# Loads of a second expert group moved ahead of a w2 load, and copies reordered in the first attention head

## The chip, the cores and the metric

One NeuronCore of a Trainium2 chip runs the whole program. The metric is the device time of one execution in microseconds (us); lower is better. The kernel before took 422.44 us (median of 3 runs, 422.02 to 424.92). The execution whose profile is read below took 423.74 us, and the span from its first to its last instruction is 421.9 us.

## The reference

Three layers are computed in a row, all in float32:

```
attention (2 x 8 heads, 768 steps, head size 64):
    state = gamma_h * state + outer(k_t, v_t);   y_t = (q_t . state) / 8
dense layer on x = y, [2, 768, 512]:
    h = relu(x @ w_in)                           # 512 -> 1024
    c = 3-tap convolution of h along the sequence, per channel
    x = (h * sigmoid(c)) @ w_out                 # 1024 -> 512
experts (8): logits = x @ w_gate, a sigmoid gate decides whether a token
    takes its own best expert or its predecessor's;
    out = p[e] * (relu(x @ w1[e]) @ w2[e])       # 512 -> 1024 -> 512
```

## The kernel before

**Attention.** Two heads share the 128 partitions, so there are 8 pairs ("heads" in the code), each cut into 6 slices of 128 steps. For each slice TensorE computes scores `s_ps` (line 284), VectorE multiplies them by a decay table into `at` (286), and two slices later TensorE adds the state (`inc`, 292) and computes the output `y` from `at` and the values `vz` (304) and from q and the state (306). Before this, `prepare` (line 244) makes operands of each head: q copied into a zero-padded tile `qz` (253 on VectorE, 255 on ScalarE), q times its decay on GpSimd (258), k times its decay (263 on VectorE for the first head's second half, 265 on ScalarE), and the values copied into the zero-padded `vz` (`values`, 279, ScalarE). Only the first head comes in two parts, slices 0 and 1 and slices 2 to 5, so that it can start before all of it is loaded. `prepare` is a generator; the main loop over slices (line 444) calls `advance`, which takes one step of each running generator when its counter comes to zero. What the loop writes first stands first in each engine's queue; the engines take their queues strictly in this order.

**Dense layer.** Its matmuls (lines 134 to 136, three passes on split high and low words) start inside the attention loop and then run on their own until 235 us.

**Experts.** Tokens are sorted by expert into tiles of 128 rows; 11 tiles are always run (`experts`, line 968). What is left over from the experts goes in groups of four quarters of 32 rows (`group`, 902), of which two are always run. For tile j, `fetch(j, 0)` loads w1 (2 MB in 4 loads of 512 KB, line 715), `fetch(j, 1)` loads w2; `cut` (732) splits the words on ScalarE (738) and VectorE (739), `g1` and `g2` multiply. For j > 1 a load carries a condition read on the chip: where the tile two before used the same expert, it moves nothing. A group needs 8 pieces of weights of 2 MB each (4 of w1, 4 of w2, each piece 4 loads, line 729), which go alternately into two slots, `qc` and `qs1l`; a piece can be loaded only when TensorE has used up what stood in its slot. `hook` (line 960) is called four times a tile, and at the numbers in `QT` it takes one step of the group; group 1 has its steps at hooks 21, 26, 30, 30, 31, 35 and 40. Hook 26 comes at the end of tile 5, hook 30 at the end of tile 6; each multiplies two pieces (924) and then asks for the next two. All weight loads are issued by the SP queue, in the order in which the loop writes them, and every load there waits until the load eight places before it has landed (eight semaphores are used in turn).

Of the kernel before, what the change touches and what calls it, by code (L numbers as in the profile page):

```python
# [92 lines left out]
def tile_kernel(ctx, tc, cat, cst, qT, kT, kN, vN, w_in, conv_w, w_out, wg, w1, w2, out):  # L93
# [116 lines left out]
    def keep_busy(n):  # L210

        for _ in range(n):
            te.matmul(idle[:, 0:P], zst[0], zst[0], start=True, stop=True)
# [9 lines left out]
    class Head:  # L223
# [21 lines left out]
        def prepare(self):  # L245
            hp = self.hp
            qd = ca[:, hp, C_QD:C_QD + CH]
            for c in self.parts:
                t = slice(c.start * CH, c.stop * CH)
                for j in range(2):  # L250
                    pj = slice(64 * j, 64 * j + 64)
                    if len(self.parts) > 1 and j:
                        ve.tensor_copy(out=self.qz[pj, j, t], in_=self.kq[pj, 1, t])  # L253
                    else:
                        se.activation(out=self.qz[pj, j, t], in_=self.kq[pj, 1, t], func=AF.Copy)
                    yield 1
                q1 = self.q1[:, c.start:c.stop]
                po.tensor_tensor(out=q1, in0=q1, in1=qd.unsqueeze(1).to_broadcast([P, len(c), CH]), op=ALU.mult)
                for j in range(2):
                    k1 = self.kv[:, 0, c.start:c.stop, 64 * j:64 * j + 64]  # L260
                    kd = ca[:, hp, C_KD + j:C_KD + j + 1]
                    if len(self.parts) > 1 and j:
                        ve.tensor_scalar(out=k1, in0=k1, scalar1=kd, scalar2=None, op0=ALU.mult)
                    else:
                        se.activation(out=k1, in_=k1, func=AF.Copy, scale=kd)
                    if len(self.parts) > 1:
                        self.values(c, j)
                    yield 1

            if len(self.parts) == 1:  # L270
                yield 1
                for c in (range(3), range(3, 6)):
                    for j in range(2):
                        self.values(c, j)
                    yield 3
# [40 lines left out]
    def load(p):  # L316
        heads[p] = Head(p // 4, p % 4, p % 2)

    def small():
        w = yield from narrow(cw_words, 24)  # L320
        se.activation(out=cw.rearrange("p m t -> p (m t)"), in_=w, func=AF.Copy)
        ve.tensor_copy(out=identr, in_=ident)
        ve.tensor_copy(out=sel, in_=cs[0:RK + E, R_SEL:R_SEL + 10])
# [95 lines left out]
    running, done = [], []  # L419

    def advance():
        for r in list(running):
            r[1] -= 1
            if r[1] <= 0:
                r[1] = next(r[0], 0)
                if not r[1]:
                    running.remove(r)
# [6 lines left out]
    start = heads[0].prepare()  # L434
    for _ in range(4):
        next(start)
    running.append([start, 1])
    rest = None
    LOOK = 2
    LOADS = {1: 2, 11: 3, 15: 4, 20: 5, 28: 6, 32: 7}  # L440
# [3 lines left out]
    for i in range(len(seq) + LOOK):  # L444
        if i < len(seq):
            p, c = seq[i]
            heads[p].scores(c)
            if i == 0:
                keep_busy(8)
            if c == 0 and p + 1 < 8:  # L450
                running.append([heads[p + 1].prepare(), 2])
            if i in STARTS:
                running.append([convert(*parts.pop(0)), 1])
            if i in LOADS:
                load(LOADS[i])
            if i == 14:
                running.append([small(), 1])
        todo = rest
        if i >= LOOK:
            p, c = seq[i - LOOK]  # L460
            rest = heads[p].output(c)
        if todo:
            todo()
        advance()
        while i >= FIRST and slices[0] < (i - FIRST + 1) * RATE:
            next(first)
            slices[0] += 1
# [227 lines left out]
    def expert_at(n):  # L695
        return sy.value_load(ei[0:1, 0, n:n + 1], min_val=0, max_val=E - 1)

    def raw(lane, which):
        if (lane, which) not in RAW:
            RAW[lane, which] = (wx if lane and which else ws).tile([P, 4, 1024], F32, name=f"r{lane}{which}")  # L700
        return RAW[lane, which]

    def fetch(j, which, parts=range(4)):

        src = (w1, w2)[which].rearrange("e p a n -> e p (a n)")
        kw = {}
        if j == 0:
            src = src[0]
        else:
            src = src[bass.ds(expert_at(j), 1)].rearrange("o p n -> (o p) n")  # L710
            if j > 1:
                kw = dict(cond=sy.value_load(ei[0:1, 1, j:j + 1], min_val=0, max_val=1), cond_hint=True)
        dst = raw(j % 2, which)
        for i in parts:
            sy.dma_start(out=dst[:, i, :], in_=src[:, i * 1024:(i + 1) * 1024], **kw)
# [120 lines left out]
    def begin_x(j):  # L836

        x, X[j] = X[j], psb.tile([P, 4, P], F32, tag="b", name="tp")
        for k in range(4):
            te.matmul(X[j][:, k, :], x[:, k * P:(k + 1) * P], ident, start=(k == 0), stop=False, skip_group_check=True)  # L840
        late_x(j, 0)
# [45 lines left out]
    def finish(j, last=False):  # L887
        if last:
            yo = wk.tile([P, F], F32, tag="hr", name="yo")[:, 0:DM]
        elif j >= NTILE:  # L890
            yo = wk.tile([P, F], F32, tag="hq", name="yo", bufs=1)[:, 0:DM]
        else:
            yo = wk.tile([P, DM], F32, name="yo", bufs=1)
        se.activation(out=yo, in_=Y.pop(j), func=AF.Copy, scale=pr[:, j:j + 1])  # L894
        po.indirect_dma_start(out=rows_of[j], out_offset=bass.IndirectOffsetOnAxis(ap=it[:, j:j + 1], axis=0),  # L895
                              in_=yo, in_offset=None, bounds_check=NT - 1, oob_is_err=False)

    def tile_g1():
        return [psa.tile([P, 512], F32, tag=f"a{n}", name="g1") for n in range(2)]
# [55 lines left out]
    QT = [3, 5, 10, 10, 11, 15, 20] + [21, 26, 30, 30, 31, 35, 40]  # L955
    groups = []
    hooks = [0]

    def hook():
        hooks[0] += 1  # L960
        while QT and QT[0] <= hooks[0]:
            QT.pop(0)
            while groups and next(groups[0], done) is done:
                groups.pop(0)

    def experts(n):

        fetch_q(0, 0, 1)
        fetch(1, 1)
        for j in range(2):  # L970
            begin_x(j)
        for j in range(2):
            turn_x(j)
        gather(NTILE)
        gather(2)
        groups.extend(group(g, g + 1 < QSTAT) for g in range(QSTAT))
        h = tile_g1()
        for i in range(2):
            g1(0, i, h)
            cut(1, 0, i)  # L980
            if i:
                relu(0, h)
            hook()
        cut(0, 1, 0)
        fetch(2, 0)
        T = {}
        for j in range(n):
            last, ahead = j + 1 == n, j + 2 < n
            behind = j + 3 < n and j > 0 and hooks[0] + 1 in QT
            if j + 3 < n and not behind:  # L990
                fetch(j + 3, 0)
            if j > 0:
                finish(j - 1)
            if j + 3 < n:
                gather(j + 3)
            if j == 2:
                gather(NTILE + 1)
            if j not in T and j > 0:
                T[j] = turn_h(j)
            if not last:  # L1000
                h = tile_g1()
                g1(j + 1, 0, h)
                if j == 0:
                    T[j] = turn_h(j)
                    cut(0, 1, 1)
                if ahead:
                    cut(j + 2, 0, 0)
                hook()
                if behind:
                    fetch(j + 3, 0)  # L1010
                g1(j + 1, 1, h)
                if ahead:
                    cut(j + 2, 0, 1)
                relu(j + 1, h)
                hook()
            if ahead:
                turn_x(j + 2)
                fetch(j + 2, 1)
            Y[j] = y = psb.tile([P, 512], F32, tag="b", name="y")
            for i in range(2):  # L1020
                g2(j, i, T[j], y)
                if not last:
                    cut(j + 1, 1, i)
                    if not ahead and i == 0:
                        T[j + 1] = turn_h(j + 1)
                    hook()
        finish(n - 1, True)
        assert not QT

# [68 lines left out]
```

## Time and profile before

| what | value |
|---|---|
| time, median of 3 runs | 422.44 us |
| time of the profiled execution | 423.74 us |
| its span | 421.9 us |
| TensorE matmul busy | 406.2 us (96%) |
| VectorE, ScalarE, GpSimd busy | 290.3, 256.1, 92.7 us |
| bytes moved by DMA | 86.57 MB |
| granted TensorE clock, mean | 0.996 |

The busy time of TensorE is modelled from the starts of its matmuls, so a matmul that waits for part of its data may still count as busy. That is why the rows below show single stretches in order of time: from one row's start to the next one's start is what the step took.

### The profile page before, as it was taken

The page shows a single profiled execution, that of the slowest core. Times are in us where ns is not written, and L with a number is a line of the kernel's source. Part 1 is how long each engine was busy: PE and PEld are TensorE (multiplying, and loading weights), DVE is VectorE, ACT ScalarE, POOL GpSimd, SP SyncE. Part 2 cuts the span into 40 slices and gives each one's busy share as a digit, 9 for nine tenths or more (in the row PEclk, how much of TensorE's full clock was granted, in tenths as well). Part 3 has the DMA queues.
Part 4 walks back from the last instruction along what each step waited for, and adds up shares of the span by engine and source line. Part 5 has one row for each costly group of instructions (what it writes and reads, how often), then busy time and mean ns, then how long its engine had stood idle before and what let it go on. Part 6 is the DMA issues. An engine that isn't in the chain of part 4 may idle for free.

```text
span 421.9 us, 7069 instructions
## 1 busy us (share of the span) xinstructions
PE 406.2 (96%) x2412; PEld 329.5 (78%) x2412; DVE 290.3 (69%) x494; ACT 256.1 (61%) x405; POOL 92.7 (22%) x92
## 2 busy tenths in 40 slices
PE   8999999999999999999999999999999998999992
PEld 7898999999987889988778886767667764676671
DVE  3789989798973621678995387968595957285550
ACT  2787778578663333667313487869586846485550
POOL 5356756230100000000004130341131320200110
PEclk9999999999999999999999999999999999999998
DMA  7989871320000101000486999999978969658301
GB/s 238 389 295 405 276 246 54 106 89 6 2 2 0 75 27 50 2 0 2 174 294 198 372 406 331 381 412 401 403 285 302 361 244 402 237 218 299 151 31 42
DMA packets 27322, 86.57 MB, mean 205 GB/s; under 512 B 3598, under 2 KB 4622, under 8 KB 27280
## 3 DMA queue, kind: packets, MB, share of 16 engines
q1 hardware_dynamic: 25200, 79.76, 51.1%
q0 software_dynamic: 2080, 6.29, 4.1%
q8 instruction: 21, 0.34, 0.3%
q14 instruction: 21, 0.17, 0.1%
HBM read 105.18 MB, written 6.55 MB: 265 GB/s over the span
## 4 chain that ended last, share of the span: by engine, by line
PE 38%; issue 34%; POOL 10%; DVE 8%; ACT 4%; DMA 3%; SPq 1%; POOLq 0%
PE x_ps L134 6%; PE x_ps L135 5%; PE x_ps L136 5%; POOL out_dram L895 4%; POOL xg L748 4%; PE h_ps L134 3%; PE y L304 3%; PE h_ps L135 3%; PE s_ps L284 3%; PE h_ps L136 3%; DVE cc L367 3%; DMA xs<-xl 2%; PE y L306 2%; DMA kq<-in_qT_dram 1%; ACT cc L364 1%
## 5 line engine op out<-in xcount | busy, mean ns | idle before, releaser
L134 PE MATMUL h_ps<-xT,wih 128*128 128x384 f32 x128 | 46.1, 360 | 0.1
L895 POOL DMA_INDIRECT out_dram<-yo,it x13 | 16.4, 1262 | 134.8 <-ACT yo L894 134.8
L367 DVE SCALAR_TENSOR_TENSOR cc<-h,cw,cc 128x768 f32<-128x768 f32 x32 | 34.9, 1091 | 15.2 <-ACT cc L364 15.1
L748 POOL DMA_INDIRECT xg<-xs,it x13 | 18.4, 1418 | 121.8 <-DVE ei L683 107.9
L135 PE MATMUL h_ps<-xT,wih 128*128 128x384 f32 x128 | 43.1, 337 | 0.0
L136 PE MATMUL h_ps<-xT,wil 128*128 128x384 f32 x128 | 43.1, 336 | 0.0
L134 PE MATMUL x_ps<-woh,hg 128*128 128x512 f32 x96 | 38.6, 402 | 0.0
L135 PE MATMUL x_ps<-wol,hg 128*128 128x512 f32 x96 | 37.5, 391 | 0.0
L136 PE MATMUL x_ps<-woh,hg 128*128 128x512 f32 x96 | 37.5, 391 | 0.0
L739 DVE TENSOR_TENSOR ws1h<-r,ws1h 128x1024 fp32r<-128x1024 f32 x22 | 26.0, 1222 | 12.8 <-ACT ws1h L738 9.3
L155 POOL TENSOR_TENSOR na<-na,raw 128x512 int32<-128x512 int32 (+1 forms) x17 | 23.0, 1354 | 50.8 <-DVE na L153 25.7
L739 DVE TENSOR_TENSOR wc<-r,wc 128x1024 fp32r<-128x1024 f32 x22 | 26.0, 1221 | 11.7 <-ACT wc L738 11.6
L738 ACT ACTIVATE wc<-r 128x1024 fp32r<-128x1024 f32 x22 | 22.1, 1055 | 14.6 <-PE g L136 14.6
L304 PE MATMUL y<-at,vz 128*128 128x128 f32 x192 | 29.5, 275 | 0.9 <-ACT vz L279 0.9
L284 PE MATMUL s_ps<-qz,kq 128*128 128x256 f32 x96 | 29.0, 385 | 1.0 <-DVE qz L253 1.0
L739 DVE TENSOR_TENSOR ws0h<-r,ws0h 128x1024 fp32r<-128x1024 f32 x22 | 26.0, 1222 | 5.6 <-ACT ws0h L738 5.5
L739 DVE TENSOR_TENSOR ws0l<-r,ws0l 128x1024 fp32r<-128x1024 f32 x22 | 26.0, 1222 | 5.1 <-ACT ws0l L738 5.0
L304 PEld LDWEIGHTS y<-at,vz 128*128 128x128 f32 x192 | 25.9, 192 | 1.5 <-ACT vz L279 1.1
L738 ACT ACTIVATE ws0l<-r 128x1024 fp32r<-128x1024 f32 x22 | 22.1, 1053 | 7.7 <-PE y L136 7.7
L286 DVE TENSOR_TENSOR at<-s_ps,ca 128x256 f32<-128x256 f32 x48 | 20.2, 421 | 8.4 <-PE s_ps L284 7.7
L134 PEld LDWEIGHTS h_ps<-xT,wih 128*128 128x128 f32 x128 | 24.1, 189 | 1.9 <-issue 1.2
L506 ACT ACTIVATE xn<-x_ps 128x512 f32<-128x512 f32 x10 | 6.0, 598 | 32.0 <-PE x_ps L136 13.8
(234 smaller groups left out, 1042.4 us busy)
## 6 DMA issues: line engine op xcount, KB each, us to landing
r<-in_w_dram SPq DMA_DIRECT2D x88, 512.0 KB
qc<-in_w_dram SPq DMA_DIRECT2D x32, 512.0 KB
qs1l<-in_w_dram SPq DMA_DIRECT2D x32, 512.0 KB
raw<-in_w_in_dram SPq DMA_DIRECT2D x8, 512.0 KB
raw<-in_w_out_dram SPq DMA_DIRECT2D x8, 512.0 KB
kq<-in_qT_dram SPq DMA_DIRECT2D x7, 384.0 KB
kq<-in_kT_dram SPq DMA_DIRECT2D x7, 384.0 KB
kv<-in_vN_dram SPq DMA_DIRECT2D x7, 384.0 KB
```

Of the source, the lines that this page charges most:

```text
L134: te.matmul(ps, lhi, rhi, start=first, stop=False)
L135: te.matmul(ps, lhi, rlo, start=False, stop=False)
L136: te.matmul(ps, llo, rhi, start=False, stop=last)
L155: po.tensor_tensor(out=a, in0=a, in1=lo, op=ALU.add)
L284: te.matmul(ps, self.kq[:, 0, tok], self.qz[:, :, tok], start=True, stop=True)
L286: ve.tensor_tensor(out=self.at[c], in0=ps, in1=self.dm, op=ALU.mult)
L304: te.matmul(y, vz[:, c, j, :], at[:, j, :], start=(j == 0), stop=(c == 0 and j == 1))
L367: ve.scalar_tensor_tensor(out=cc, in0=h[:, i:i + S], scalar=cw[:, m, i:i + 1], in1=cc, op0=ALU.mult, op1=ALU.add)
L738: se.activation(out=w[:, 0, h, :], in_=r, func=AF.Copy)
L739: ve.tensor_tensor(out=w[:, 1, h, :], in0=r, in1=w[:, 0, h, :].bitcast(F32), op=ALU.subtract)
L748: return po.indirect_dma_start(out=xg, out_offset=None, in_=xs[0:n], in_offset=bass.IndirectOffsetOnAxis(ap=it[:, j:j + 1], axis=0), bound ...
L895: po.indirect_dma_start(out=rows_of[j], out_offset=bass.IndirectOffsetOnAxis(ap=it[:, j:j + 1], axis=0), in_=yo, in_offset=None, bounds_ch ...
```

## The change

Three edits. In `experts`, the w2 load of tile j + 2 is put behind the second multiplication of tile j where only the second group is left and its next step falls on the hook after the next one. That is so for tiles 5 and 6 (hooks 26 and 30), so `fetch(7, 1)` and `fetch(8, 1)` move. In `prepare`, the two copies of values of the first head stand ahead of its k times decay. In the main loop, the two copies of q of the first head's second part are taken right after the first scores instead of after the first and the second slice; the counter 3 keeps the later steps where they were.

```
-    running.append([start, 1])
+    running.append([start, 3])
...
             if i == 0:
                 keep_busy(8)
+                for _ in range(2):
+                    next(start)
...
                 po.tensor_tensor(out=q1, in0=q1, in1=qd.unsqueeze(1).to_broadcast([P, len(c), CH]), op=ALU.mult)
+                for j in range(2 if len(self.parts) > 1 else 0):
+                    self.values(c, j)
                 for j in range(2):
...
-                    if len(self.parts) > 1:
-                        self.values(c, j)
                     yield 1
...
             if ahead:
                 turn_x(j + 2)
-                fetch(j + 2, 1)
+                after = len(groups) == 1 and hooks[0] + 1 not in QT and hooks[0] + 2 in QT
+                if not after:
+                    fetch(j + 2, 1)
...
                     hook()
+            if ahead and after:
+                fetch(j + 2, 1)
```

The SP queue at tile 5, before: `r00` is w1 of tile 8, `r11` is w2 of tile 7, `qc4` and `qs1l` are the third and fourth w1 piece of group 1, `r10` is w1 of tile 9. The TENSOR_LOADs read the expert and the condition.

```order
L715 DMA r00_2027<-in_w1_dram 128x1024
L696 TENSOR_LOAD ei_1427
L696 ISA x2
L712 TENSOR_LOAD ei_1427
L712 ISA x2
L715 ISA
L715 DMA r11_2465<-in_w2_dram 128x1024
...
L729 DMA qc4_3689<-in_w1_dram 128x1024
...
L729 DMA qs1l_3702<-in_w1_dram 128x1024
...
L715 DMA r10_2037<-in_w1_dram 128x1024
```

The same place with the change:

```order
L717 DMA r00_2027<-in_w1_dram 128x1024
L731 ISA
L731 DMA qc4_3667<-in_w1_dram 128x1024
...
L731 DMA qs1l_3680<-in_w1_dram 128x1024
...
L698 TENSOR_LOAD ei_1427
L698 ISA x2
L714 TENSOR_LOAD ei_1427
L714 ISA x2
L717 ISA
L717 DMA r11_2465<-in_w2_dram 128x1024
...
L717 DMA r10_2037<-in_w1_dram 128x1024
```

The four loads of `r11` moved behind the eight loads of the two pieces. At tile 6 the four loads of `r01` (w2 of tile 8) move likewise.

ScalarE in the first head, before (`qz_104` and `qz_105` belong to the first and the second head; 2x64 and 4x64 are the first and the second part):

```order
L255 ACTIVATE qz_104<-kq 64x512
L255 ACTIVATE qz_105<-kq 64x768
L265 ACTIVATE kv<-kv,ca 128x4x64
L279 ACTIVATE vz<-kv 128x4x64
L255 ACTIVATE qz_105<-kq 64x768
L311 ACTIVATE xT<-y 128x256
L279 ACTIVATE vz<-kv 128x4x64
```

With the change:

```order
L255 ACTIVATE qz_104<-kq 64x512
L255 ACTIVATE qz_105<-kq 64x768
L279 ACTIVATE vz<-kv 128x4x64 x2
L267 ACTIVATE kv<-kv,ca 128x4x64
L255 ACTIVATE qz_105<-kq 64x768
L311 ACTIVATE xT<-y 128x256
```

Both copies of values now stand ahead of k times decay; before, the second one stood behind another head's copy and an output.

VectorE in the first head, before:

```order
L263 TENSOR_SCALAR kv<-kv,ca 128x2x64
L286 TENSOR_TENSOR at<-s_ps,ca 128x256 x2
L253 COPY qz_104<-kq 64x512
L286 TENSOR_TENSOR at<-s_ps,ca 128x256
L297 COPY st_108<-inc 64x64 x2
```

With the change:

```order
L265 TENSOR_SCALAR kv<-kv,ca 128x2x64
L286 TENSOR_TENSOR at<-s_ps,ca 128x256
L253 COPY qz_104<-kq 64x512
L286 TENSOR_TENSOR at<-s_ps,ca 128x256 x2
L297 COPY st_108<-inc 64x64 x2
```

The copy of q's second part now stands ahead of the second slice's scores times decay.

## Rows read from the trace of the kernel before

**Rows 1.** Windows: stretch, its length, busy us (count) by engine, clock, DMA share, GB/s
```profile
15.00:45.00 30.00, 28.90 (x208) 26.84 (x207) 27.11 (x80) 22.35 (x51) 16.84 (x13) 1.00 0.92 335
340.00:363.00 23.00, 21.54 (x100) 12.22 (x99) 11.42 (x11) 10.97 (x15) 1.99 (x3) 1.00 0.81 305
```

**Rows 2.** Timeline of PE, hooks 30 and 35: start, us, what [idle before]
```profile
352.84 1.83 PE L924 MATMUL hq_ps<-qc,xq 128*32 128x512 f32 x6
354.89 1.48 PE L924 MATMUL hq_ps<-qc,xq 128*32 128x512 f32 x9 [0.22 <-DMA qc<-in_w_dram]
...
358.20 2.15 PE L924 MATMUL hq_ps<-qs1l,xq 128*32 128x512 f32 x4 [0.98 <-DMA qs1l<-in_w_dram]
360.55 1.90 PE L924 MATMUL hq_ps<-qs1l,xq 128*32 128x512 f32 x10 [0.20 <-DMA qs1l<-in_w_dram]
362.38 1.09 PE L826 MATMUL tp<-cs,hr 128*128 128x128 f32 x8
...
366.07 1.03 PE L826 MATMUL tp<-cs,hq 128*128 128x128 f32 x8
...
379.32 1.92 PE L946 MATMUL yq_ps<-qc,tq 128*32 128x512 f32 x16
...
382.89 0.50 PE L134 MATMUL g<-wc,xh 128*128 128x512 f32 x1
```

**Rows 3.** Waits of PEld, whole run: total us, times, longest
```profile
PEld hq_ps L924 <- DMA qs1l<-in_w_dram: 5.0, 5, 1.9
```

**Rows 4.** Timeline of SP's issues, tiles 4 to 6
```profile
327.79 15.01 SPq L715 DMA_DIRECT2D r<-in_w_dram  x12
343.09 2.44 SPq L729 DMA_DIRECT2D qc<-in_w_dram  x4
345.79 4.29 SPq L729 DMA_DIRECT2D qs1l<-in_w_dram  x4
```

**Rows 5.** Tile r on SP, windows 327:339.5 and 340:343: ns min/median/max, first and last start
```profile
L715 SPq DMA_DIRECT2D r<-in_w_dram x8: 73/73/84, 327.8 to 338.7; - x8
...
L715 SPq DMA_DIRECT2D r<-in_w_dram x4: 311/341/387, 340.4 to 342.5; - x4
```

**Rows 6.** Timeline of ACT around hook 30
```profile
352.94 2.00 ACT L738 ACTIVATE ws0l<-r 128x1024 fp32r<-128x1024 f32 x2 [0.55 <-PE y L136]
362.49 1.09 ACT L930 ACTIVATE hq<-hq_ps 128x512 f32<-128x512 f32 x2 [7.54 <-PE hq_ps L924]
363.46 0.69 ACT L894 ACTIVATE yo<-y,pr 128x512 f32<-128x512 f32 x1
```

**Rows 7.** The page's GB/s in 40 slices of 10.55 us
```profile
GB/s 238 389 295 405 276 246 54 106 89 6 2 2 0 75 27 50 2 0 2 174 294 198 372 406 331 381 412 401 403 285 302 361 244 402 237 218 299 151 31 42
```

**Rows 8.** Timeline of PE, first head
```profile
9.27 0.67 PE L284 MATMUL s_ps<-qz,kq 128*128 128x256 f32 x2 [1.02 <-DVE qz L253]
...
12.48 0.46 PE L292 MATMUL inc<-kv 128*128 128x128 f32 x2
...
14.10 0.49 PE L304 MATMUL y<-at,vz 128*128 128x128 f32 x2 [0.94 <-ACT vz L279]
...
14.65 0.60 PE L284 MATMUL s_ps<-qz,kq 128*128 128x256 f32 x2
```

**Rows 9.** Timeline of DVE, first head
```profile
8.74 0.42 DVE L253 COPY qz<-kq 64x512 f32<-64x512 f32 x1
```

**Rows 10.** Timeline of ACT, first head
```profile
7.82 0.63 ACT L255 ACTIVATE qz<-kq 64x512 f32<-64x512 f32 x1 [1.06 <-DMA kq<-in_qT_dram]
10.78 0.84 ACT L255 ACTIVATE qz<-kq 64x768 f32<-64x768 f32 x1 [2.34 <-DMA kq<-in_qT_dram]
11.54 0.49 ACT L265 ACTIVATE kv<-kv,ca 128x256 f32<-128x256 f32 x1
11.93 0.40 ACT L279 ACTIVATE vz<-kv 128x256 f32<-128x256 f32 x1
```

**Rows 11.** Timeline of SP, the load that waits for k's second part
```profile
8.49 0.33 SPq L431 DMA_DIRECT2D cs<-in_cst_dram  x1
```

## The prediction

> **What bounds the kernel now.** I read the windows first. TensorE is busy 28.90 of 30 us between 15 and 45 us [rows 1], and the same holds, with the clock at 1.00, up to 340 us: TensorE is the bound, and the others keep up. What delays TensorE at one place therefore delays the end by the same, unless a later wait takes it back. So I then looked for places where TensorE waits. The waits of TensorE and of its weight loads name a DMA into `qs1l` as the largest, 5.0 us in 5 waits [rows 3]; the window from 340 to 363 holds most of it (21.54 busy of 23, and weight loads at 12.22) [rows 1]. The timeline shows it plainly. At hook 30 the two pieces are multiplied from 352.84 to 362.38, which is 9.54 us. At hook 35 the same number of matmuls of the same shape takes 382.89 - 379.32 = 3.57 us [rows 2]. So **5.97 us are lost at hook 30**, and the idle gaps beside these rows (0.22, 0.98, 0.20) hide most of it, because a matmul that has started counts as busy. The rows also tell what it waits for: the last load of `qc` lets it go on at 354.89, loads of `qs1l` at 358.20 and 360.55.
>
> Why are these pieces late? The SP queue issues them at 343.09 and 345.79 [rows 4]. Ahead of them stand twelve tile loads. Eight take 73 to 84 ns to issue and the last four 311 to 387 ns [rows 5]; the eight move nothing (their expert is the one already there), and the four, from 340.4, are w2 of tile 7. So from 340.4 on twelve loads of 512 KB are under way, 6.3 MB; w2 goes first, and the pieces land behind it.
>
> In the first head TensorE waits twice: 1.02 us before the third scores, for VectorE's copy of q, and 0.94 us (from 13.16 to 14.10) for ScalarE's copy of values [rows 8].
>
> **The change, part by part.** *The w2 load of tile 7.* Without it in front, SP reaches the first piece right after the last of the eight empty loads, 338.7 [rows 5], plus 0.4 for one issue: 339.1. Its slot is free then, because hook 26 has used `qc` up by 338; `qs1l` is free at 340.4, before its turn. Now the landings, by count, from the twelve loads of the trace: the 8th (last of `qc`) is seen at 354.89, 14.5 us after the first issue at 340.4; the 10th at 358.20, 17.8 us; the 12th at 360.55, 20.15 us [rows 2, 5]. With the change the eight piece loads come first, so the last lands at 339.1 + 14.5 = 353.6. The matmuls of the second piece begin at 352.84 + 1.8 (half of 3.57) = 354.6. So both pieces are there, with 1 us to spare, and the step takes 3.57 us: it ends at 356.4 instead of 362.38. **Gain 5.97.**
>
> What is late next is w2 itself. Its last load lands at 339.1 + 20.15 = 359.25. It is needed for a multiplication only some 8 us after hook 30, but its `cut` stands in ScalarE's queue ahead of the group's `hq`, of tile 6's output `yo` and of all the rest. Before, that cut ran at 352.94 [rows 6]. Now its second half starts at 359.25 and takes 1.0; then `hq` 1.09 and `yo` 0.69 [rows 6]: 362.0. TensorE meanwhile does transposes and the first half of tile 8, 3.69 us (362.38 to 366.07 [rows 2]), to 360.1, and wants to transpose `hq`. The second four transposes, 0.4 later, need the PSUM bank that `yo` empties (four banks go round). So TensorE waits from 360.5 to 362.0: **loss 1.5**. Bounds for this loss: 0 if w2 lands by 357.8, since 1.5 less is wanted; 3 if it lands as much later than reckoned. I take 1.5, which the count of landings gives. VectorE's half of the cut ends by 361.6 and stays hidden, as do the extra transposes of tile 7's h.
>
> The Trainium skill (DMA: Bandwidth & Descriptors, Anatomy of one DMA) fits a DMA as about 2.0 us plus its bytes over 436 GB/s. For these 6.3 MB that is an estimate of 16.4 us where the rows have 20.15; by it w2 would land at 355.5, the loss would vanish, and the sum below would be 6.7. The rows decide; the page is for a queue other than SP's.
>
> *The w2 load of tile 8* (moved at hook 30) has the same condition as the empty loads: the issues of tiles 6 and 8 moved nothing [rows 5]. Nothing is transferred, so it costs and brings nothing, and the pieces for hook 35 are issued some 6 us earlier.
>
> *q's copies.* VectorE's copy now runs when q's second part has landed, 7.82 (there ScalarE starts its own [rows 10]), and takes 0.42 [rows 9], to 8.24; ScalarE's ends at 8.45; k's second part has landed by 8.49, since SP's load there waits for it [rows 11]. So the third scores start at 8.55 instead of 9.27: 0.7 sooner. GpSimd's multiply follows by as much. Scores of the second slice times decay come at 8.29 as before, behind the copy.
>
> *Copies of values.* ScalarE's order is now two copies, then k times decay, all behind the second head's q copy that ends at 11.6 [rows 10]. At about 0.4 and 0.4, then 0.49, k's product ends at 12.85, so `inc`, at 12.48 before [rows 8], comes at 12.9. The second copy of values is then long there, and the wait to 14.10 goes. From `inc` to the second pair of `y` it takes 0.5 to 0.7, and from there to the next scores 14.65 - 14.10 = 0.55. These scores start between 13.9 and 14.15 instead of 14.65: a gain of 0.5 to 0.8 in all, not the sum of both waits, because a new wait of about 1.4 us on k's product takes the place of the second. I take **0.7**. It is kept, for up to 340 us everything is started by TensorE's progress; VectorE at 27.11 of 30 us [rows 1] may cost some of it.
>
> **Sum.** 5.97 - 1.5 + 0.7 = 5.2 us. From the profiled execution's 423.74 that is 418.5; that run lies 1.3 above the median of 422.44, so against the median **417.2 us**.
>
> **Rivals.**
> 1. *The order of issue does not matter*, since 16 engines share all loads that are under way; the pieces then land as late as before, and only the first head gains: 422.44 - 0.7 = 421.7. Against it: the landings in the trace follow the order of issue, 354.89, 358.20, 360.55. The Trainium skill (same page, Queues, rings and completion order) says that a ring's descriptors are consumed in order but that completion is not first in, first out; the first half is what the rows show. 6%.
> 2. *The new wait on w2 is larger*, by 1.2 to 3.5 us, as ScalarE stands still in order and every us of w2's delay after 357.8 is a us of TensorE's: 418.4 to 420.7, say 419.5. For it: SP has only eight loads under way, and w2's wait for landings of pieces. 14%.
> 3. *Slower than before.* The same stop of ScalarE, from the point where w2's last load lands after 364.4 (5.2 us later than reckoned). It would if the loads ran at the 244 GB/s of the slice from 337.5 to 348 [rows 7]: 6.3 MB take 25.8 us, with 2 for the rest 27.8, so 366.9 and a loss of 7.65 more: 424.9. Against it: that slice holds idle stretches; from 340 to 363 the mean is 305 GB/s [rows 1], which gives 20.6 us, as counted. 3%.
> 4. *More than forecast*: w2 lands early enough, nothing is lost, and the first head gains 0.8 to 1.5: 414.8 to 415.5. 7%.
>
> **How the numbers follow.** The forecast, 415.6 to 418.4, has 70%; what remains is in the rivals. The likeliest case gives 417.2. The range from 415.3 to 419.4 holds the forecast, about half of rival 2 and some of rival 4, some 80%. A measurement of this kernel tells about 1% from no change, so faster means below 418.2 and slower above 426.7: faster 0.75 (forecast nearly whole, rival 4), within 1% 0.23, slower 0.02.
>
> **What would show it.** In the profile after: hook 30's pair of pieces in about 3.6 us with no DMA wait, SP issuing `qc` at about 339 and w2 of tile 7 after both pieces; ScalarE's second cut of w2 at about 358 to 360 ended by a DMA; a TensorE wait of about 1.5 us before the second transposes of `hq`, released by `yo`; the third scores at 8.5 and `inc` at 12.9 released by ScalarE's k product (all late times earlier by the head's gain). Hook 30 still at 9 us would make rival 1 right. A wait for w2 by the multiplication itself, or pieces late at hook 35, would show steps that I left out.

## The result: about 1% faster, with 4.4 us gained in the profiled execution where 5.2 were forecast

The changed kernel took **418.88 us** (median of 8 runs, 417.41 to 421.46) beside 422.69 us for the kernel before (8 runs, 422.02 to 424.92). The ratio on record is 0.9893, with a 95% interval of 0.9868 to 0.9918; the quotient of the two medians is 0.9910, which is 3.8 us. The forecast was 417.2 us, in a range from 415.3 to 419.4: the median lies in the range, 1.7 us above the forecast. The profiled execution took 419.32 us, its span is 417.5 us, and the mean granted clock is 0.993. Against the profiled execution of before (423.74 us, span 421.9) that is 4.4 us less, where 5.2 were forecast.

### The profile page after: what moved, and what is told of

The parts are those of the page before. It is cut to its first block, busy times and chain, and to the rows that moved or that the text cites. A ratio compares the mean times of both kernels' runs of the same rounds, so it can differ in the third digit from the quotient of the medians.

```text
span 417.5 us, 7069 instructions
## 1 busy us (share of the span) xinstructions
PE 401.6 (96%) x2412; PEld 328.9 (79%) x2412; DVE 290.2 (69%) x494; ACT 256.4 (61%) x405; POOL 93.8 (22%) x92
## 4 chain that ended last, share of the span: by engine, by line
PE 39%; issue 33%; POOL 10%; DVE 8%; ACT 4%; DMA 3%; SPq 1%; POOLq 0%
PE x_ps L134 6%; PE x_ps L136 5%; PE x_ps L135 5%; POOL xg L750 4%; POOL out_dram L897 4%; PE h_ps L134 3%; PE y L304 3%; PE h_ps L135 3%; PE s_ps L284 3%; PE h_ps L136 3%; DVE cc L367 3%; PE y L306 2%; DMA xs<-xl 2%; DMA kq<-in_qT_dram 2%; ACT cc L364 1%
## 5 line engine op out<-in xcount | busy, mean ns | idle before, releaser
L750 POOL DMA_INDIRECT xg<-xs,it x13 | 19.6, 1509 | 121.2 <-DVE ei L685 107.6
L134 PE MATMUL h_ps<-xT,wih 128*128 128x384 f32 x128 | 46.1, 360 | 0.1
L897 POOL DMA_INDIRECT out_dram<-yo,it x13 | 16.4, 1263 | 130.1 <-ACT yo L896 130.1
L740 ACT ACTIVATE ws0h<-r 128x1024 fp32r<-128x1024 f32 x22 | 22.3, 1064 | 7.7 <-DMA r<-in_w_dram 5.4
```

The lines of the kernel that those rows point to most:

```text
L134: te.matmul(ps, lhi, rhi, start=first, stop=False)
L740: se.activation(out=w[:, 0, h, :], in_=r, func=AF.Copy)
L750: return po.indirect_dma_start(out=xg, out_offset=None, in_=xs[0:n], in_offset=bass.IndirectOffsetOnAxis(ap=it[:, j:j + 1], axis=0), bound ...
```

## The profile after

First the windows that answer to [rows 1]. The columns are the same; the last row is a stretch that the prediction passed over.

```profile
15.00:45.00 30.00, 28.89 (x207) 26.86 (x207) 27.39 (x81) 23.41 (x53) 17.56 (x14) 1.00 0.91 336
...
340.00:363.00 23.00, 21.59 (x124) 15.39 (x124) 12.03 (x12) 13.38 (x19) 2.42 (x4) 1.00 1.00 383
...
230.00:300.00 70.00, 68.89 (x399) 50.89 (x398) 48.71 (x48) 48.27 (x63) 17.17 (x16) 1.00 0.99 378
```

From 340 to 363 us TensorE runs 124 matmuls instead of 100 in the same 23 us, and weight loads are busy for 15.39 us instead of 12.22. TensorE's busy time (21.59 and 21.54) says nothing about it, because a matmul that waits half-way counts as busy: **count the matmuls, not the busy share**. The DMA engines are now full in that stretch (1.00 and 383 GB/s, before 0.81 and 305).

The timeline of TensorE around hook 30 answers to [rows 2]:

```profile
352.54 1.92 PE L926 MATMUL hq_ps<-qc,xq 128*32 128x512 f32 x16
354.28 1.90 PE L926 MATMUL hq_ps<-qs1l,xq 128*32 128x512 f32 x16
356.11 1.09 PE L828 MATMUL tp<-cs,hr 128*128 128x128 f32 x8
...
360.96 0.66 PE L828 MATMUL tp<-cs,hq 128*128 128x128 f32 x4 [1.00 <-ACT hq L932]
362.03 0.66 PE L828 MATMUL tp<-cs,hq 128*128 128x128 f32 x4 [0.41 <-ACT yo L896]
362.44 0.48 PE L134 MATMUL g<-wc,xh 128*128 128x512 f32 x1
```

The pair of pieces is multiplied in 356.11 - 352.54 = 3.57 us without a wait, where it took 9.54. The new wait stands behind it, where the prediction put it: the eight transposes of `hq` came in one piece before, and now come in two halves, the first released by ScalarE's `hq`, the second by `yo`.

What ScalarE did meanwhile, answering to [rows 6]:

```profile
355.61 2.26 ACT L740 ACTIVATE ws0h<-r 128x1024 fp32r<-128x1024 f32 x2 [5.40 <-DMA r<-in_w_dram]
358.19 2.24 ACT L740 ACTIVATE ws0l<-r 128x1024 fp32r<-128x1024 f32 x2 [0.32 <-DMA r<-in_w_dram]
360.33 1.07 ACT L932 ACTIVATE hq<-hq_ps 128x512 f32<-128x512 f32 x2
361.29 0.69 ACT L896 ACTIVATE yo<-y,pr 128x512 f32<-128x512 f32 x1
```

The wait before each half of w2's cut is now ended by a DMA. ScalarE stood idle for 5.40 us for the first half. `hq_ps` was there from about 356 on, but `hq` was copied only at 360.33, behind both halves. The cut's last instruction ran from about 359.4 (the row's end less one instruction of 1.06), `hq` and `yo` behind it.

The issues of SP, answering to [rows 4, 5]:

```profile
327.43 11.01 SPq L717 DMA_DIRECT2D r<-in_w_dram  x8
338.68 1.96 SPq L731 DMA_DIRECT2D qc<-in_w_dram  x4
340.89 2.54 SPq L731 DMA_DIRECT2D qs1l<-in_w_dram  x4
345.32 8.15 SPq L717 DMA_DIRECT2D r<-in_w_dram  x8
```

The pieces are issued from 338.68 instead of 343.09, and w2 of tile 7 behind them. The last row holds w2's four loads, which move data, and four empty ones of w1 of tile 9.

Of the waits of the weight loads over the whole run, what is left of the largest one, answering to [rows 3] (5.0 us in 5 waits):

```profile
PEld hq_ps L926 <- DMA qs1l<-in_w_dram: 0.8, 1, 0.8
```

The first head, TensorE, answering to [rows 8]:

```profile
9.17 0.67 PE L284 MATMUL s_ps<-qz,kq 128*128 128x256 f32 x2 [0.96 <-DVE at L286]
...
13.28 0.49 PE L292 MATMUL inc<-kv 128*128 128x128 f32 x2 [1.00 <-ACT kv L267]
...
14.27 0.60 PE L284 MATMUL s_ps<-qz,kq 128*128 128x256 f32 x2
```

And VectorE and ScalarE there, answering to [rows 9, 10]:

```profile
8.27 0.42 DVE L253 COPY qz<-kq 64x512 f32<-64x512 f32 x1 [1.69 <-DMA kq<-in_qT_dram]
8.72 0.42 DVE L286 TENSOR_TENSOR at<-s_ps,ca 128x256 f32<-128x256 f32 x1
```

```profile
11.37 0.85 ACT L255 ACTIVATE qz<-kq 64x768 f32<-64x768 f32 x1 [2.47 <-DMA kq<-in_qT_dram]
12.12 0.70 ACT L279 ACTIVATE vz<-kv 128x256 f32<-128x256 f32 x2
12.73 0.49 ACT L267 ACTIVATE kv<-kv,ca 128x256 f32<-128x256 f32 x1
```

The third scores come only 0.10 sooner. `inc` is later than before (13.28, before 12.48) and waits for ScalarE's k times decay; the wait for the copy of values is gone; the sixth slice's scores start at 14.27 instead of 14.65. One thing is not the change's doing: in this execution q's second part landed at 8.27 and the second head's q at 11.37, where before had 7.82 and 10.78.

**The balance by stretches.** Hook 30 starts 0.30 us sooner than before (352.54 and 352.84): that is what the head and all else up to there brought. From there to the first `g` on `wc`, the second half of tile 8, it takes 362.44 - 352.54 = 9.90 us. From hook 30's start to the first transpose of `hq` it took 366.07 - 352.84 = 13.23 before [rows 2]. Experiment 2 below runs this stretch without any wait in 7.27, and to the first `g` in 8.06. So 13.23 - 7.27 = 5.96 were to be had, and 9.90 - 8.06 = 1.84 of it were not got: 0.30 + 5.96 - 1.84 = 4.42, which is the 4.4 us between the spans.

## The experiments

The ratios are to the kernel before on the same chip, with 95% intervals, as they are on record; the quotient of two medians differs from them by up to 0.003. The median of the kernel before was 423.25 us beside experiments 1 and 2, and 423.73 us beside experiments 3 and 4. Each kernel is told as a difference from the changed kernel, unless said otherwise.

**1. Which of the three edits does it.** Three kernels. The first has only the moved w2 loads, with the head as before. The second has only the head's copies, with w2 where it was:

```
-                after = len(groups) == 1 and hooks[0] + 1 not in QT and hooks[0] + 2 in QT
-                if not after:
-                    fetch(j + 2, 1)
+                fetch(j + 2, 1)
...
-            if ahead and after:
-                fetch(j + 2, 1)
```

The third has the head's copies and moves the w2 load of tile 8 alone:

```
-                after = len(groups) == 1 and hooks[0] + 1 not in QT and hooks[0] + 2 in QT
+                after = j == 6
```

Expected of the w2 loads alone:

> Only the two moved w2 loads, the first head as before. Theory (the pieces of hook 30 no longer queue behind w2 of tile 7): hook 30 takes 3.6 us instead of 9.5, TensorE then loses about 1.7 us behind ScalarE, so about 4.2 us faster than before, and the first 16 us as before. Rival (the gain is the first head's, or comes from a shift of everything): under 1 us faster.

Expected of the head alone:

> Only the copies of the first head, the loads as before. Theory: 0.3 to 0.8 us faster than before, hook 30 still takes 9 to 9.5 us. Rival (the first head gives as much as the loads): 2 us or more faster.

Expected of tile 8's w2 alone:

> As the change, but only w2 of tile 8 is moved (hook 30), w2 of tile 7 stays ahead of the pieces. Theory: that load moves nothing, so hook 30 still takes 9 to 9.5 us and the time is that of the first head's edits alone, 0.3 to 0.8 us faster than before. Rival (each moved load brings part of the gain): about 2 us faster than before, hook 35 shorter.

Measured: the w2 loads alone 419.61 us, ratio 0.9898 [0.9858, 0.9938]; the head alone 424.22 us, 1.0008 [0.9977, 1.0039]; head and tile 8's w2 423.88 us, 0.9983 [0.9949, 1.0016]. So the w2 load of tile 7 carries the result, and the others can't be told from nothing in a whole run. In the profile of the w2 loads alone the first 16 us were not as before: TensorE's clock fell there (last section), so hook 30 starts later than in the kernel before, and the steps themselves have to be compared. TensorE at hook 30, with the w2 loads alone:

```profile
354.63 1.92 PE L924 MATMUL hq_ps<-qc,xq 128*32 128x512 f32 x16
356.37 1.90 PE L924 MATMUL hq_ps<-qs1l,xq 128*32 128x512 f32 x16
358.20 1.09 PE L826 MATMUL tp<-cs,hr 128*128 128x128 f32 x8
362.90 0.65 PE L826 MATMUL tp<-cs,hq 128*128 128x128 f32 x4 [0.84 <-ACT hq L930]
```

and with tile 8's alone:

```profile
354.75 1.85 PE L926 MATMUL hq_ps<-qc,xq 128*32 128x512 f32 x6
...
362.83 1.90 PE L926 MATMUL hq_ps<-qs1l,xq 128*32 128x512 f32 x10 [0.22 <-DMA qs1l<-in_w_dram]
364.66 1.09 PE L828 MATMUL tp<-cs,hr 128*128 128x128 f32 x8
```

The first takes 3.57 us and has the new wait behind it; the second takes 9.91, about as before (9.54). **The order of issue decides whether the pieces are there in time**: the same twelve loads are under way in both. To stand first is also to be issued sooner (`qc` at 338.68 instead of 343.09), and no run separates the two. The first rival (order does not matter) falls, and tile 8's w2, which moves no data, brings nothing, as the prediction had it.

**2. Is the new loss ScalarE's stop behind w2?** If so, it goes when the two cuts of w2 of tile 7 are taken out of ScalarE's way, with nothing changed in the loads. This kernel takes them one tile later, behind `hq` and `yo`:

```
+                if j == 7:
+                    for i in range(2):
+                        cut(j, 1, i)
                 if ahead:
                     cut(j + 2, 0, 0)
...
-                    cut(j + 1, 1, i)
+                    if j != 6:
+                        cut(j + 1, 1, i)
```

> As the change, and the two cuts of tile 7's w2 stand in ScalarE's and VectorE's queue behind hq, tile 6's output and tile 7's split h instead of ahead of them. Theory (TensorE's 1.7 us wait before the transposes of hq comes from ScalarE standing in order behind w2's landing): the wait goes, hq is copied at about 356 to 357, and the kernel is 1.7 us faster than the change. Rival (what costs it is w2's landing itself, wanted by tile 7's multiplication): no faster, the wait stands before tile 7's y.

Measured: 417.26 us (415.05 to 418.67), ratio 0.9848 [0.9798, 0.9898]; span 415.2 us. TensorE at hook 30:

```profile
352.11 1.92 PE L926 MATMUL hq_ps<-qc,xq 128*32 128x512 f32 x16
...
355.68 1.09 PE L828 MATMUL tp<-cs,hr 128*128 128x128 f32 x8
...
359.38 1.03 PE L828 MATMUL tp<-cs,hq 128*128 128x128 f32 x8
360.17 0.48 PE L134 MATMUL g<-wc,xh 128*128 128x512 f32 x1
```

and ScalarE:

```profile
355.81 1.09 ACT L932 ACTIVATE hq<-hq_ps 128x512 f32<-128x512 f32 x2 [6.03 <-PE hq_ps L926]
356.79 0.69 ACT L896 ACTIVATE yo<-y,pr 128x512 f32<-128x512 f32 x1
357.36 1.10 ACT L832 ACTIVATE th<-tp 128x512 fp32r<-128x512 f32 x2
358.31 2.04 ACT L740 ACTIVATE ws0h<-r 128x1024 fp32r<-128x1024 f32 x2
```

The eight transposes of `hq` are in one piece again, without a wait. From hook 30's start to the first `g` it takes 8.06 us instead of 9.90. `hq` now follows `hq_ps` at once, at 355.81 instead of 360.33, and the cut of w2 starts at 358.31, with no wait for a landing in its row. So the whole loss of 1.84 us came from the cut standing in order ahead of `hq`, behind a load that TensorE did not need yet. The same shows in other runs: this stretch takes 9.72 to 9.95 us in the four profiles that move the load and not the cuts, and 8.06 in the three that move both. This version is clearly faster than the kernel before. That it is also faster than the changed kernel is shown by this stretch; in whole runs the two intervals overlap (0.9868 to 0.9918 and 0.9798 to 0.9898).

**3. Which of the head's edits does what.** One kernel has the values' copies in the new place and q's copies in the old; the other the reverse. Each was run once, for its profile.

```
-    running.append([start, 3])
+    running.append([start, 1])
...
-                for _ in range(2):
-                    next(start)
```

That was the edit of the first; the second put the two lines with `self.values(c, j)` back behind k times decay.

> As the change, but q's copies of the first head where they were before; only the copies of values are ahead of k times decay. Theory (what sets the first head's end is ScalarE's copy of the second head's q, ahead of k's product in its queue, so q's earlier copies are taken back at inc): inc comes 1.9 us after that copy starts and the scores of the sixth slice 2.9 us after it, as with the change. Rival (q's copies give their 0.7 us): these scores 3.6 us after it.

> As the change, but the copies of values where they were before; only q's copies are earlier. Theory: the scores of the sixth slice come 3.9 us after ScalarE's copy of the second head's q starts, as in the kernel before, the second copy of values releasing the second pair of y. Rival: 3.2 us after it.

Measured: 420.49 and 418.12 us, one run each, beside 423.73 us; single runs can't be ranked here. TensorE's head, with the values' copies alone:

```profile
8.35 0.60 PE L284 MATMUL s_ps<-qz,kq 128*128 128x256 f32 x2
9.97 0.67 PE L284 MATMUL s_ps<-qz,kq 128*128 128x256 f32 x2 [1.02 <-issue]
...
14.14 0.60 PE L284 MATMUL s_ps<-qz,kq 128*128 128x256 f32 x2
```

and with q's copies alone:

```profile
8.25 0.67 PE L284 MATMUL s_ps<-qz,kq 128*128 128x256 f32 x2 [0.60 <-DMA kq<-in_kT_dram]
...
11.75 0.49 PE L292 MATMUL inc<-kv 128*128 128x128 f32 x2 [0.40 <-ACT kv L265]
...
13.76 0.49 PE L304 MATMUL y<-at,vz 128*128 128x128 f32 x2 [1.22 <-DMA kv<-in_kN_dram]
...
14.31 0.60 PE L284 MATMUL s_ps<-qz,kq 128*128 128x256 f32 x2
```

In the last row of `y` a DMA is named as releaser; it is ScalarE's second copy of values, which ended at 13.71, just ahead of 13.76.

The landings differ from execution to execution, so I count from a point that the order on ScalarE hangs on: its copy of the second head's q, which starts when that has landed. From there to the sixth slice's scores it takes 14.65 - 10.78 = 3.87 us before [rows 8, 10], and 14.31 - 10.45 = 3.86 with q's copies alone. It takes 14.27 - 11.37 = 2.90 with both, 2.91 with the head alone (11.03 to 13.94) and in experiment 2 (10.88 to 13.79), and 3.16 with the values' copies alone (10.98 to 14.14). **So both edits together bring 0.97 us here, the values' copies alone 0.71, and q's copies alone nothing (0.01).** Each figure is from one execution. Counted from the landing of q's second part, q's copies do bring the third scores sooner: 9.27 - 7.82 = 1.45 us before, 9.17 - 8.27 = 0.90 with the change, 8.25 - 7.46 = 0.79 with q's copies alone. But `inc` then waits for ScalarE's k times decay (0.40 and 1.00 us in the rows), and without the values' copies the wait before `y` follows. With the values' copies alone `inc` came at 13.18, which is 2.20 us after the start of ScalarE's copy and not the 1.9 expected: the third scores were late (9.97, because the second scores had been late, at 8.35, and VectorE's copy of q stood behind their product with the decay), and VectorE's half of k times decay, later in the same queue, ended at 12.96, after ScalarE's (12.84). That cost 3.16 - 2.90 = 0.26 us at the sixth slice.

**4. Is there more in the head, and does it count?** `inc` waits for k times decay, which stands behind the second head's q on ScalarE. With the counter at 2 instead of 3 the step is taken one slice sooner and stands ahead of it. This was tried on top of experiment 2's kernel, and that kernel was run again beside it on the same chip:

```
-    running.append([start, 3])
+    running.append([start, 2])
```

> As the change with late cuts of w2, and the first head's second copies of values and its k product stand ahead of the second head's q copy in ScalarE's queue (and k's other half a slice earlier on VectorE). Theory: inc no longer waits, it comes 0.4 to 0.5 us after the fifth scores start, at 11 to 12 instead of 12.8 to 13.3, and the first head ends 1.2 to 1.9 us earlier; of it 0 to 1.5 us stay in the time beside the late cuts alone. Rival (the next load, of the second head, holds it up): inc is early but the gap comes at the second head, no gain by 20 us.

> The late cuts once more, on the same chip as the run with the early head. Theory: 1.7 us faster than the change, some 6 us faster than the kernel before, hook 30's step 3.6 us and no wait before the transposes of hq. Rival: as the change, 4 to 4.5 us faster than before.

Measured: 416.66 us, ratio 0.9836 [0.98, 0.9873], with the early head; 417.16 us, 0.984 [0.9797, 0.9882], without it. TensorE's head with it:

```profile
11.40 0.39 PE L292 MATMUL inc<-kv 128*128 128x128 f32 x2
...
12.30 0.60 PE L284 MATMUL s_ps<-qz,kq 128*128 128x256 f32 x2
```

Both waits are gone, and the sixth slice's scores start at 12.30 (13.60 without it), 1.3 us sooner, of which the run's time shows 0.5, within the intervals. Much of the lead goes early, so the rival was right in part: the eleventh slice's scores start at 18.92 and 19.78, a lead of 0.86 us, and in the last head 0.55 us are left (77.45 and 78.00). Then the comparison is disturbed. Without the early head TensorE's granted clock fell to 0.50, the lower of its two levels, from 96 to 98 us. Over 20 us that reads 0.91 (length, TensorE's busy us, clock, DMA share, GB/s):

```profile
80.00:100.00 20.00, 19.55 (x137) 0.91 0.19 53
```

With the early head it stayed at 1.00, and the lead is 1.96 us at 127 us, of which some 1.4 are the clock's and not the head's. TensorE at the first and at the third pair of pieces of the first group, with the early head:

```profile
251.95 1.92 PE L926 MATMUL hq_ps<-qc,xq 128*32 128x512 f32 x16
...
292.45 1.92 PE L948 MATMUL yq_ps<-qc,tq 128*32 128x512 f32 x16
...
296.03 1.90 PE L948 MATMUL yq_ps<-qs1l,tq 128*32 128x512 f32 x10 [0.22 <-DMA qs1l<-in_w_dram]
297.86 0.50 PE L134 MATMUL g<-wc,xh 128*128 128x512 f32 x1
```

and without it:

```profile
253.88 1.90 PE L926 MATMUL hq_ps<-qc,xq 128*32 128x512 f32 x13
...
298.31 0.50 PE L134 MATMUL g<-wc,xh 128*128 128x512 f32 x1
```

A lead of 253.88 - 251.95 = 1.93 us at the first pair is down to 0.45 behind the third. Against experiment 2's profile, which has the same kernel without the fall of the clock, the lead is 0.92 at the first pair (252.87) and 0.67 behind the third (298.53). The kernel that is ahead meets loads of `qs1l` that have not landed: with the early head the second pair, up to the transposes of its `hq`, takes 279.19 - 270.72 = 8.47 us and without it 279.92 - 272.65 = 7.27, and the third pair takes 297.86 - 292.45 = 5.41 us (5.13 without it) for a step that takes 3.57 when its pieces are there. From 230 to 300 us the DMA engines are full (0.99 in the window of after above; 1.00 before), so TensorE meets the landings there, and these differ between executions. From the first pair to behind the third, the ten profiles of this study take 43.2 to 46.1 us. That spread hides a few tenths of a head, and why the landings differ was not settled.

## Why the prediction was right

- **Hook 30.** Forecast: 9.54 us become 3.57, a gain of 5.97. It was 3.57 in each of the seven kernels that move tile 7's w2, and 9.58 and 9.91 in the two that don't. The reason (pieces behind w2 in SP's order) is shown by experiment 1. The last piece was forecast to land at 353.6. SP's empty loads behind w2 wait for the loads of `qs1l` eight places before them, and the fourth of them, which waits for the last one, is issued at 353.40, so the last piece was there by then.
- **The loss behind ScalarE.** Mechanism and place were right, and shown by experiment 2. The forecast put w2's last load at 359.25 and the end of the wait at 362.0; the profile has about 359.4 and 362.03. The size was off, 1.84 instead of 1.5, because TensorE came to the wait 0.30 sooner than reckoned: it finished the pair at 356.11, not 356.4. The prediction then added the head's gain on top, "all late times earlier by the head's gain", but w2 did not land earlier. From the first issue to the start of the last cut it took 359.4 - 338.68 = 20.7 us, with 20.15 counted from the trace of before. By the fit of the Trainium skill (DMA: Bandwidth & Descriptors, Anatomy of one DMA) the estimate for these bytes was 16.4 us, by which the loss would vanish; the 20.7 us measured decide against it here.
- **The head.** This is the other term that was mis-sized: 0.7 forecast, 0.38 at the sixth slice and 0.30 at hook 30 in this profile. The forecast of `inc` at 12.9, released by k times decay, was right in kind; it came at 13.28 because the second head's q landed 0.59 later. Counted from that landing the head gains 0.97 (experiment 3); the prediction took a landing time of one execution for a fixed one. The third scores were forecast at 8.55 and came at 9.17: q landed 0.45 later, and they were released not by the copy but by the second slice's scores times decay (8.72 to 9.14), which the edit put behind the copy. The prediction had left that product at 8.29 and had not reckoned with the third scores waiting for it.
- **"It is kept, for up to 340 us everything is started by TensorE's progress."** This step holds for the profile of after (0.38 at the head, 0.30 at hook 30), but not in general: in experiment 4 a lead of 1.30 us was down to 0.55 in the last head, and one of 1.93 us, mostly the clock's, shrank to 0.45 between 252 and 298 us, where the DMA engines are full and TensorE waits for landings. That stretch stood in the page of before [rows 7], and I did not read it.
- **Sum.** 5.96 - 1.84 + 0.30 = 4.42 us, forecast 5.97 - 1.5 + 0.7 = 5.2. Both errors have the same sign, so no error hid another.
- **Rivals.** That the order does not matter: fell (experiment 1). That the wait on w2 is larger by 1.2 us or more: it was larger by 0.34. Slower: no w2 load landed after 364.4 in the kernels that move it. More than forecast: not with this change; with the cuts moved too it was 423.25 - 417.26 = 6.0 us by the medians. (From the prediction's own terms this rival's times come to 415.0 to 415.7, not 414.8 to 415.5.)

## What to carry to other kernels

When a load is moved behind others, look for the first instruction that reads it in every engine's order, not for the place where its result is needed: here a cut on ScalarE stood waiting for words that TensorE read some 8 us after they were cut (357.87 to 365.62), and 1.84 of 5.96 us went back until the cut moved with its load. Don't add two gains that meet at the same landing: what comes sooner to a wait that a DMA ends only waits longer. And before counting on a lead of TensorE, look for the stretch with full DMA engines between it and the end. Before calling a difference between two profiles a lead, compare the granted clock in the stretches before it.

## What the runs showed of the hardware

- The order of issue on SP's queue shows in the landings when twelve loads of 512 KB are under way: the eight loads of the two pieces ahead of w2's four, or behind them, changed the pair at hook 30 by 6 us, with DMA busy shares of 0.81 before and 1.00 after.
- With the w2 loads alone, TensorE's granted clock fell in the first head, though nothing had changed there against before. The windows of TensorE (length, busy us, clock, DMA share, GB/s) just behind its two waits (0.38 us ahead of `inc` and 1.23 us ahead of `y`):

```profile
14.00:16.00 2.00, 1.86 (x7) 0.56 1.06 386
16.00:18.00 2.00, 2.00 (x11) 0.58 1.03 395
```

  The mean lies near the lower of the two levels (1.2 of 2.4 GHz). The pair of scores took 1.06 us at 15.07, and 0.60 otherwise; from the released `y` to the seventh slice's scores it took 17.63 - 14.14 = 3.49 us, before 15.97 - 14.10 = 1.87, so about 1.6 us were lost. Before had nearly the same waits (0.94 us ahead of `y`) and no such fall.
- In three other profiles (the head alone, the values' copies alone, the late cuts run again) the clock was 0.91 from 80 to 100 us, with 0.50 from 96 to 98, while TensorE was busy for 19.5 of the 20 us; other profiles had the same busy time and no fall. It is 1.4 to 1.5 us in a kernel where differences of 0.5 us are discussed. In the profile of the head alone it ate the head's gain: the seventh slice's scores start at 15.26 (15.97 before), but the first matmul of the dense layer's second product (`x_ps`) at 127.32 (126.61 before). What set these falls off was not settled.
